# A decode block on one core: 21 tiny probe loads on SP's queue and three 17-partition loads issued by GpSimd

## The chip, the cores and the metric

The kernel runs on one core of one Trainium2 chip. The time is device microseconds of one execution. Before the change the median of two runs is 185.91 us (185.82 and 186.01). Traces come from one profiled execution; times inside it count from the start of its span.

## The reference

One block of a transformer at decode: two sequences, one token each, 640 channels, modulated by a condition `c`. In short:

```python
mod = silu(c) @ w_mod                      # (2,640) @ (640,3840): sa, ca, ga, sb, cb, gb
h = layernorm(x) * (1 + ca) + sa
q = h @ wq                                 # 32 heads of 192
k, v = k_cache[:, :, -1024:], v_cache[:, :, -1024:]
o = softmax(q @ k.T * 192 ** -0.5) @ v
x = x + ga * (o @ wo)
h = layernorm(x) * (1 + cb) + sb
x = x + gb * ((gelu(h @ w_gate) * (h @ w_up)) @ w_down)
```

All tensors are bf16. With one token a sequence, every weight and every cached key and value is used once. The kernel reads 76.88 MB: `w_mod` 4.9 MB, `wq` and `wo` 7.9 MB each, keys and values 25.2 MB each, and 5.9 MB for the feed-forward part.

## The kernel before, in words

All big loads go into one buffer of 128 partitions, `arena`, at places written out by hand (`place`, with `tiles` for the pieces of the caches; `HS` is half a slot of 64 x 192 elements). They are issued on SP's queue in this order: `w_mod`; `wq`; for sequence 0 the K tiles 0 and 1 (64 positions a partition) and 2 (128 positions), V tile 0; K tile 0 of sequence 1; V tile 1 of sequence 0; K tile 1 of sequence 1; the two V tiles of sequence 1; `wo`; `w_gate`; `w_up`; and `w_down` in three parts of 8, 3 and 1 rows. The function `pump` issues the next load as soon as every earlier load that overlaps it in `arena` has been consumed, so an SP issue waits on the semaphore of the engine that reads the old contents. The first load is moved ahead of the program's opening barrier. A load puts 128 rows on the DMA engines, 8 rows an engine, one packet a row (38 to 61 KB for the big ones).

The computation follows the loads. `w_mod` gives the modulation (L454), `wq` the queries (L486), which are copied to all partitions (`qbc`). For each K tile DVE multiplies 16 positions at a time with the query (L512, `d_mul`), PE sums over channels through an identity matrix (L524, `p_reduce`), and DVE ends the sums (L531, `c_sum`). The softmax (L537 to L554) is followed by `weights_v`: DVE spreads the weights of 64 positions over the 32 heads into one of the two halves of `Em` (L561), and PE multiplies them with the V tile (L575, `p_pv`). After the last V tile come the selection of heads (L616), a row of matmuls into an unused bank that keep the clock up (`keep_clock`, L408, which read `Em`), `wo` (L634), the second layer norm, `w_gate` and `w_up` (L655), and `w_down` (L675), whose three parts each wait for their own load. Two DVE operations (L681, L683) make the output, and ACT issues the store (L685). SP waits for the store at the end (L698).

GpSimd sets up constants in the first 7.3 us (memsets and masks; the last are the `zsel` selects, L374) and does nothing after. ACT issues two small loads at the start: `c` (2 partitions of 1280 bytes) and `x` (8 partitions of 320 bytes). All issues pass through the helper `k_dma`, so all have line L290 in the profile.

Dependences are tracked by key: `S.op` and `S.dma` take lists of keys read and written, and `resolve` turns them into semaphore waits, of which it leaves out those that an earlier wait of the same engine covers. Each engine runs its list in order.

`Em` (128 partitions, 2 x 64 x 32 bf16) is written for the first time by L561, at 87.85 us in the trace.

Of the kernel before, what the change touches and what calls it, by code (L numbers as in the profile page):

```python
# [8 lines left out]
BF16 = mybir.dt.bfloat16  # L9
# [110 lines left out]
def bass_adaLN_cond__sliding_block_cached__geglu_ffn__decode_kernel(  # L120
# [51 lines left out]
    WD_SPLIT = [(0, 8), (8, 3), (11, 1)]  # L172
# [15 lines left out]
    with es:  # L188
        S = _Sched(nc, es)
        sb = lambda name, shape, dt: es.enter_context(nc.sbuf_tensor(name, shape, dt))  # L190
# [10 lines left out]
        for kind, b, t, z in tiles:  # L201
            j0, n = (K_SPLIT if kind == "k" else V_SPLIT)[b][t]
# [25 lines left out]
        maskE = sb("maskE", [P, H], BF16)  # L228
# [29 lines left out]
        Em = sb("Em", [P, 2, JE, H], BF16)  # L258
# [22 lines left out]
        def bank(k):  # L281
            return ("bank", k)
# [6 lines left out]
        def k_dma(dst, src):  # L289
            return lambda e: e.dma_start(dst, src)  # L290

        items = list(place)
        assert items[0] == ("wm", 0)
        queue = {"next": 0, "done": set(), "ops": {}}

        def overlap(x, y):
            (a, m), (b, n) = place[x], place[y]
            return a < b + n and b < a + m

        def keys(it, lo=0, width=None):  # L300
            o, n = place[it]
            width = n - lo if width is None else width
            assert lo + width <= n
            return [("ar", z) for z in range((o + lo) // UNIT, -(-(o + lo + width) // UNIT))]

        def view(it, lo=0, width=None):
            o, n = place[it]
            width = n - lo if width is None else width
            return arena[:, o + lo:o + lo + width]

        def source(it):
            kind = it[0]
            if kind == "wm":
                return w_mod.rearrange("(p k) n -> p (k n)", k=KT)
            if kind == "wq":
                k0, n = WQ_SPLIT[it[1]]
                return A_wq.rearrange("(p k) n -> p (k n)", k=KT)[:, k0 * NQ:(k0 + n) * NQ]
            if kind == "wo":
                t0, n = WO_SPLIT[it[1]]
                return A_wo.rearrange("(p t) n -> p (t n)", t=NT)[:, t0 * D:(t0 + n) * D]  # L320
            if kind == "wg":
                return B_w_gate.rearrange("(p k) n -> p (k n)", k=KT)
            if kind == "wu":
                k0, nk = WU_SPLIT[it[1]]
                return B_w_up.rearrange("(p k) n -> p (k n)", k=KT)[:, k0 * F:(k0 + nk) * F]
            if kind == "wd":
                r0, nr = WD_SPLIT[it[1]]
                return B_w_down.rearrange("(p r) n -> p (r n)", r=FC)[:, r0 * D:(r0 + nr) * D]
            b, (j0, n) = it[1], span[it]
            src = A_k_cache if kind == "k" else A_v_cache  # L330
            return src[b][:, K0:Sk, :].rearrange("h (x j) d -> h x j d", x=XQ)[:, :, j0:j0 + n, :].rearrange("h x j d -> h x (j d)")

        def pump(*consumed):
            queue["done"].update(consumed)
            while queue["next"] < len(items):
                n = queue["next"]
                it = items[n]
                if not all(x in queue["done"] for x in items[:n] if overlap(x, it)):
                    break
                queue["ops"][it] = S.dma("sp", k_dma(view(it), source(it)), sem_of[it], writes=keys(it), name="ld_%s" % "_".join(str(z) for z in it))  # L340
                queue["next"] += 1

        pump()
        wm_dma = queue["ops"][("wm", 0)]
        S.op("pool", lambda e: e.memset(xr[:, :], 0.0), writes=["xr"], name="xr0")
# [4 lines left out]
        for nm, t in (("scT", scT), ("oT", oT)):  # L350
# [6 lines left out]
             reads=["ones_f"], writes=["ident_f"], name="ident_f")  # L357
        S.op("pool", lambda e: e.tensor_copy(out=ident_b[:, :], in_=ident_f[:, :]),
             reads=["ident_f"], writes=["ident_b"], name="ident_b")
        S.op("pool", lambda e: e.memset(aT[:, 0:RB], 0.0), writes=["aT0"], name="aT0")  # L360
        S.op("pool", lambda e: e.memset(selq[:, :, :], 0.0), writes=["selq"], name="selq0")
        for b in range(B):
# [4 lines left out]
                 reads=["ones_b"], writes=[("selt", b)], name="selt%d" % b)  # L367
            S.op("pool", lambda e, b=b: e.tensor_copy(out=selq[:, b, :].rearrange("p (u x) -> p u x", x=SQW)[:, :, 0:P].rearrange("p u (i v) -> p u i v", i=NR)[:, :, :, 0:XQ],
                                                      in_=selt[:, b, :].rearrange("p (i x) -> p i x", x=XQ).unsqueeze(1).broadcast_to([P, HB, NR, XQ])),
                 reads=[("selt", b), "selq"], writes=["selq"], name="selq%d" % b)  # L370
        S.op("pool", lambda e: e.memset(scl[:, :], SCALE), writes=["scl"], name="scl")
        S.op("pool", lambda e: e.memset(zsel[:, :, :], 0.0), writes=["zsel"], name="zsel0")
        for i in range(2):
            S.op("pool", lambda e, i=i: e.affine_select(out=zsel[:, :, :], in_=zsel[:, :, :], pattern=[[-P, 2], [-1, ZW]],  # L374
                                                        compare_op=ALU.not_equal, fill=1.0, base=DD - 1 - 2 * P * i, channel_multiplier=DD),
                 reads=["zsel"], writes=["zsel"], name="zsel%d" % (i + 1))

        S.op("dve", lambda e: e.memset(ps[:, 0:4, :], 0.0), writes=[bank(k) for k in range(4)], name="init_Q")
        S.op("dve", lambda e: e.memset(ps[:, 6:8, :], 0.0), writes=[bank(k) for k in range(6, 8)], name="init_O")
        S.op("dve", lambda e: e.tensor_reduce(out=mask_h[:, :], in_=ident_f[:, :].rearrange("p (h x) -> p h x", x=XQ), axis=AX.X, op=ALU.add),  # L380
             reads=["ident_f"], writes=["mask_h"], name="mask_h")
        S.op("dve", lambda e: e.tensor_reduce(out=st32[:, :], in_=ident_f[:, :].rearrange("p (i m) -> p m i", m=32), axis=AX.X, op=ALU.add),
             reads=["ident_f"], writes=["st32"], name="st32")
        S.op("dve", lambda e: e.tensor_reduce(out=halfsel[:, :], in_=st32[:, :].rearrange("p (h m) -> p h m", h=2), axis=AX.X, op=ALU.add),
             reads=["st32"], writes=["halfsel"], name="halfsel")
# [3 lines left out]
             reads=["st32"], writes=["selstat"], name="selstat")  # L389
# [3 lines left out]
        def c_T(e):  # L393
            last = None
            for j in range(KT):
# [4 lines left out]
             reads=[bank(BK_T)], writes=["scT"], name="silu")  # L400
        S.op("dve", lambda e: e.tensor_copy(out=X[:, :], in_=xr[:, :]),  # L401
             reads=["xr"], writes=["X"], name="x_f32")
# [26 lines left out]
        def ln_mod(tag, opc_idx, s_idx, dst_bf):  # L429
# [15 lines left out]
             reads=["mask_h"], writes=["maskc"], name="maskc")  # L445
        S.op("dve", lambda e: e.tensor_copy(out=maskE[:, :], in_=mask_h[:, :]), reads=["mask_h"], writes=["maskE"], name="maskE")

        for half in range(2):
            def f(e, half=half):
                last = None  # L450
                for k in range(KT):
# [9 lines left out]
                 reads=[bank(half)], writes=[("modR", half)], name="mod%d_evac" % half)  # L461
            S.op("dve", lambda e, half=half: e.tensor_scalar(out=opc[:, half, :], in0=modR[:, 3 * half + 1, :], scalar1=1.0, scalar2=None, op0=ALU.add),  # L462
                 reads=[("modR", half)], writes=[("opc", half)], name="opc%d" % half)
            if half == 0:
                ln_mod("ln1", 0, 0, hT)
        pump(("wm", 0))

        def out_rows(src, key, dst_t, name):
# [9 lines left out]
        for w, (k0, nk) in enumerate(WQ_SPLIT):  # L478
            def f(e, w=w, k0=k0, nk=nk):
                last = None  # L480
                wv = view(("wq", w)).rearrange("p (k i n) -> p k i n", k=nk, i=NR)
                for kk in range(nk):
                    k = k0 + kk
                    for n in range(NQB):
                        for i in range(NR):
                            last = e.matmul(ps[32 * i:32 * i + B, n, :], lhsT=hT[:, k, 0:RM:RB], rhs=wv[:, kk, i, n * QW:(n + 1) * QW],  # L486
                                            start=(k == 0), stop=(k == KT - 1), tile_position=(0, 32 * i))
                return last
            S.op("pe", f, reads=["ln1_out"] + keys(("wq", w)), writes=[bank(n) for n in range(NQB)], name="q1_%d" % w)
            pump(("wq", w))  # L490
        for n in range(NQB):
            if n % 2 == 0:
                S.op("act", lambda e, n=n: e.activation(out=qrow[:, n * QW:(n + 1) * QW], in_=ps[:, n, :], func=ACTF.Copy),
                     reads=[bank(n)], writes=[("qrow", n)], name="q1_evac%d" % n)
            else:
                S.op("dve", lambda e, n=n: e.tensor_copy(out=qrow[:, n * QW:(n + 1) * QW], in_=ps[:, n, :]),  # L496
                     reads=[bank(n)], writes=[("qrow", n)], name="q1_evac%d" % n)
        for b in range(B):
            def f(e, b=b):
                last = None  # L500
                for u in range(HB):
# [5 lines left out]
                 reads=[bank(BK_T + b)], writes=[("qbc", b)], name="q2_evac%d" % b)  # L507
# [49 lines left out]
        def weights_v(it):  # L557
            b, (j0, n) = it[1], span[it]
            for j in range(j0, j0 + n, JE):
                z = j // JE % 2  # L560
                S.op("dve", lambda e, z=z, j=j: e.tensor_tensor(out=Em[:, z, :, :], in0=E_sb[:, b, j:j + JE].unsqueeze(2).broadcast_to([P, JE, H]),  # L561
                                                                in1=maskE[:, :].unsqueeze(1).broadcast_to([P, JE, H]), op=ALU.mult),
                     reads=[("E", b), "maskE"], writes=[("Em", z)], name="Em%d_%d" % (b, j))

        def p_pv(it):
            b, (j0, n) = it[1], span[it]
# [19 lines left out]
        for n, it in enumerate(tiles):  # L586
            kind, b, t = it
# [24 lines left out]
        def p_sel(e):  # L612
            last = None
            for dd in range(DD):
# [10 lines left out]
             reads=[bank(BK_OT), "oT"], writes=["oT"], name="oT")  # L625
# [3 lines left out]
        def wo_f(e):  # L629
            last = None  # L630
            wv = view(("wo", 0)).rearrange("p (t i n) -> p t i n", t=NT, i=NR)
            for t in range(NT):
# [9 lines left out]
             reads=[bank(2), ("modR", 0)], writes=["lnt"], name="ga_attn")  # L642
        S.op("dve", lambda e: e.tensor_tensor(out=X[:, :], in0=lnt[:, :], in1=X[:, :], op=ALU.add),
             reads=["lnt", "X"], writes=["X"], name="x1")
# [4 lines left out]
        def ffn_gu(bk, wv, name, splits):  # L649
            for ci, (k0, nk, key) in enumerate(splits):  # L650
# [11 lines left out]
             reads=[bank(0)], writes=["gl"], name="gelu")  # L662
# [3 lines left out]
             reads=[bank(1), "gl"], writes=["aR"], name="geglu")  # L666
        S.op("dve", lambda e: e.transpose(aT[:, RB:RB + FC * 32], aR[:, :]), reads=["aR"], writes=["aT"], name="aT")
        for ci, (r0, nr) in enumerate(WD_SPLIT):
            def f(e, r0=r0, nr=nr):
# [12 lines left out]
             reads=[bank(BK_OT), "go"], writes=["fin"], name="gb_y")  # L682
        S.op("dve", lambda e: e.tensor_tensor(out=finb[:, :], in0=fin[:, :], in1=xo[:, :], op=ALU.add),  # L683
             reads=["fin", "xo"], writes=["finb"], name="outR")
        S.dma("act", k_dma(out[:, 0, :].rearrange("b (u n) -> u b n", n=OC), finb[0:P:SB, :]),  # L685
              sem_out, reads=["finb"], name="st_out")
# [9 lines left out]
        del body[n0:]  # L696
        body[entry:entry] = moved
        S.emit("sp", nc.sync, tail=lambda e: e.wait_ge(sem_out, 16))  # L698
        S.emit("pool", nc.gpsimd)
        S.emit("act", nc.scalar)  # L700
        S.emit("dve", nc.vector)
        S.emit("pe", nc.tensor)
# [42 lines left out]
```

## Time and profile before

| what | value |
|---|---|
| median of 2 runs | 185.91 us (185.82, 186.01) |
| span of the profiled execution | 184.6 us (the page gives no other time of it) |
| DVE, PE, PE weight loads, ACT, GpSimd busy | 107.3, 106.4, 28.9, 14.4, 6.1 us |
| mean granted TensorE clock | 0.884 |
| HBM read | 76.88 MB, 417 GB/s over the span |
| DMA packets | 2495, of which 310 under 512 bytes |
| code fetches seen on the DMA engines | six of 16 KB on queue 8, one of 8 KB on queue 14 in the span |

A busy share is an average over stages with different limits, so the stages are looked at one by one. A DMA share of 1.00 says that all 16 engines had a packet in hand all the time. The chain of waits is followed back from the last instruction: at each step it names what released the work, which can be a transfer that itself had waited its turn behind others.

### The profile page before, as it was taken

The page shows a single profiled execution, that of the slowest core. Times are in us where ns is not written, and L with a number is a line of the kernel's source. Part 1 is how long each engine was busy: PE and PEld are TensorE (multiplying, and loading weights), DVE is VectorE, ACT ScalarE, POOL GpSimd, SP SyncE. Part 2 cuts the span into 40 slices and gives each one's busy share as a digit, 9 for nine tenths or more (in the row PEclk, how much of TensorE's full clock was granted, in tenths as well). Part 3 has the DMA queues.
Part 4 walks back from the last instruction along what each step waited for, and adds up shares of the span by engine and source line. Part 5 has one row for each costly group of instructions (what it writes and reads, how often), then busy time and mean ns, then how long its engine had stood idle before and what let it go on. Part 6 is the DMA issues. An engine that isn't in the chain of part 4 may idle for free.

```text
span 184.6 us, 1862 instructions
## 1 busy us (share of the span) xinstructions
PE 106.4 (58%) x960; PEld 28.9 (16%) x693; DVE 107.3 (58%) x105; ACT 14.4 (8%) x27; POOL 6.1 (3%) x23
## 2 busy tenths in 40 slices
PE   0019000948663096662499665946662499898833
PEld 0012000120000000001260001500001356405213
DVE  6022200049993488965993999489975838300631
ACT  2041100050000000001000000000001000220410
POOL 8400000000000000000000000000000000000000
PEclk9999955699999859999589999999998559999995
DMA  8999998999898989899898989898999999979991
GB/s 292 492 496 426 426 426 357 442 426 488 368 501 352 501 362 501 384 460 469 384 490 366 490 362 490 373 490 373 479 405 447 506 443 426 426 316 403 434 376 40
DMA packets 2495, 76.99 MB, mean 417 GB/s; under 512 B 310, under 2 KB 440, under 8 KB 568
## 3 DMA queue, kind: packets, MB, share of 16 engines
q1 hardware_dynamic: 2448, 76.87, 97.1%
q8 instruction: 6, 0.10, 0.2%
q10 hardware_dynamic: 40, 0.01, 0.0%
q14 instruction: 1, 0.01, 0.0%
HBM read 76.88 MB, written 0.00 MB: 417 GB/s over the span
## 4 chain that ended last, share of the span: by engine, by line
DMA 58%; DVE 24%; PE 16%; ACT 1%; issue 1%; SPq 0%
DMA arena<-in_A_k_cache_dram 36%; DMA arena<-in_B_w_down_dram 14%; DVE arena L512 14%; PE ps L575 8%; DMA arena<-in_w_mod_dram 8%; DVE S_sb L531 6%; PE ps L524 3%; DVE Em L561 2%; PE ps L454 2%; PE ps L675 1%; DVE negm L541 1%; ACT E_sb L549 1%; PE ps L552 1%; PE ps L545 0%; DVE M L537 0%
## 5 line engine op out<-in xcount | busy, mean ns | idle before, releaser
L524 PE MATMUL ps<-arena,ident_b 128*128 128x512 bf16 x192 | 48.9, 395 | 29.2 <-DVE arena L512 29.2
L512 DVE TENSOR_TENSOR arena<-arena,qbc 128x3072 bf16<-128x3072 bf16 x32 | 54.8, 1750 | 10.2 <-DMA arena<-in_A_k_cache_dram 8.5
L575 PE MATMUL ps<-arena,Em 128*64 128x384 bf16 x256 | 26.1, 374 | 5.6 <-DVE Em L561 5.6
L531 DVE TENSOR_REDUCE S_sb<-ps 128x32 f32<-128x1024 f32 x16 | 19.5, 1218 | 7.1 <-PE ps L524 7.1
L575 PEld LDWEIGHTS ps<-arena,Em 128*64 128x64 bf16 x256 | 16.2, 126 | 30.7 <-DVE Em L561 22.0
L561 DVE TENSOR_TENSOR Em<-E_sb,maskE 128x2048 bf16<-128x2048 bf16 x8 | 18.0, 2282 | 3.9 <-PE ps L575 3.9
L486 PE MATMUL ps<-arena,hT 128*2 128x512 bf16 x60 | 5.1, 517 | 14.0 <-DMA arena<-in_A_wq_dram 14.0
L496 DVE CAST qrow<-ps 128x512 bf16<-128x512 f32 x1 | 0.7, 691 | 17.4 <-PE ps L486 17.4
L539 PEld LDWEIGHTS ps<-ident_f,M 128*1 128x1 f32 x2 | 0.2, 79 | 61.1 <-DVE M L537 61.1
L408 PE MATMUL ps<-Em,ident_b 128*128 128x512 bf16 x41 | 9.3, 379 | 0.0
L641 DVE TENSOR_TENSOR lnt<-ps,modR 128x160 f32<-128x160 f32 x1 | 0.3, 323 | 12.7 <-PE ps L634 12.7
L549 ACT ACTIVATE E_sb<-S_sb,nbias 128x256 bf16<-128x256 f32 x2 | 1.0, 507 | 66.7 <-DVE nbias L547 66.7
L454 PE MATMUL ps<-arena,scT 128*17 128x480 bf16 x40 | 4.2, 602 | 2.1 <-DMA arena<-in_w_mod_dram 2.1
L582 ACT ACTIVATE On<-ps,rden 128x384 bf16<-128x384 f32 x2 | 1.2, 580 | 49.2 <-PE ps L575 49.2
L634 PEld LDWEIGHTS ps<-arena,oT 128*17 128x17 bf16 x192 | 3.3, 91 | 7.4 <-DMA arena<-in_A_wo_dram 7.4
L396 PE MATMUL ps<-ident_b,crow 2*128 2x2 bf16 x5 | 0.4, 177 | 6.5 <-DMA crow<-in_c_dram 6.5
L634 PE MATMUL ps<-arena,oT 128*17 128x160 bf16 x192 | 3.5, 233 | 0.6 <-DMA arena<-in_A_wo_dram 0.6
L417 PE MATMUL ps<-st,selstat 128*128 128x2 f32 x4 | 0.9, 298 | 4.9 <-ACT sqj L413 4.9
L401 DVE CAST X<-xr 128x160 f32<-128x160 bf16 x1 | 0.2, 243 | 5.8 <-DMA xr<-in_A_x_dram 5.8
L486 PEld LDWEIGHTS ps<-arena,hT 128*2 128x2 bf16 x20 | 0.6, 110 | 18.4 <-issue 18.4
L462 DVE TENSOR_SCALAR opc<-modR 128x160 f32<-128x160 f32 x2 | 0.5, 244 | 4.7 <-ACT modR L459 4.7
L655 PE MATMUL ps<-arena,h2T 128*9 128x384 bf16 x40 | 2.0, 326 | 1.9 <-DMA arena<-in_B_w_up_dram 1.3
(86 smaller groups left out, 51.1 us busy)
## 6 DMA issues: line engine op xcount, KB each, us to landing
arena<-in_A_v_cache_dram SPq DMA_DIRECT2D x4, 6144.0 KB, 26.3
arena<-in_A_k_cache_dram SPq DMA_DIRECT2D x3, 6144.0 KB, 37.5
arena<-in_A_wq_dram SPq DMA_DIRECT2D x1, 7680.0 KB, 31.5
arena<-in_A_wo_dram SPq DMA_DIRECT2D x1, 7680.0 KB, 29.2
arena<-in_A_k_cache_dram SPq DMA_DIRECT2D x2, 3072.0 KB, 42.2
arena<-in_w_mod_dram SPq DMA_DIRECT2D x1, 4800.0 KB, 14.2
arena<-in_B_w_gate_dram SPq DMA_DIRECT2D x1, 1920.0 KB, 21.2
arena<-in_B_w_up_dram SPq DMA_DIRECT2D x1, 1920.0 KB, 22.8
```

What stands on the lines that cost most here:

```text
L408: last = e.matmul(ps[:, BK_T, :], lhsT=ident_b[:, :], rhs=Em[:, 0, 0:512 // H, :].rearrange("p j h -> p (j h)"), start=True, stop=True)
L454: last = e.matmul(ps[32 * i:32 * i + RM, half, 0:MH].rearrange("p (m n) -> p m n", n=DR), lhsT=scT[:, k, :], rhs=wv[:, 3 * half:3 * half + ...
L486: last = e.matmul(ps[32 * i:32 * i + B, n, :], lhsT=hT[:, k, 0:RM:RB], rhs=wv[:, kk, i, n * QW:(n + 1) * QW], start=(k == 0), stop=(k == K ...
L512: S.op("dve", lambda e: e.tensor_tensor(out=kt, in0=kt, in1=qbc[:, b, :].unsqueeze(1).broadcast_to([P, JC, Dh]), op=ALU.mult), reads=[("qb ...
L524: last = e.matmul(o_ap, lhsT=ident_b[:, :], rhs=kt[:, :, t * GC:(t + 1) * GC], start=(t == 0), stop=(t == NCH - 1))
L531: S.op("dve", lambda e: e.tensor_reduce(out=S_sb[:, b, 2 * JC * pair:2 * JC * (pair + 1)], in_=ps[:, 2 * z:2 * z + 2, :].rearrange("p k (j ...
L541: S.op("dve", lambda e: e.tensor_reduce(out=negm[:, b, :].rearrange("p (h x) -> p h x", x=XQ), in_=ps[0:1, BK_T, 0:P].rearrange("p (h x) - ...
L549: S.op("act", lambda e: e.activation(out=E_sb[:, b, :], in_=S_sb[:, b, :], func=ACTF.Exp, scale=SCALE, bias=nbias[:, b:b + 1], accum_out=d ...
L561: S.op("dve", lambda e, z=z, j=j: e.tensor_tensor(out=Em[:, z, :, :], in0=E_sb[:, b, j:j + JE].unsqueeze(2).broadcast_to([P, JE, H]), in1= ...
L575: last = e.matmul(ps[64 * i:64 * i + 2 * H, BK_O, 0:ON], lhsT=Em[:, z, 2 * jp:2 * jp + 2, :].rearrange("p j h -> p (j h)"), rhs=view(it, l ...
L634: last = e.matmul(ps[32 * i:32 * i + RM, 2, 0:DR], lhsT=oT[:, t, :], rhs=wv[:, t, i, :], start=(t == 0), stop=(t == NT - 1), tile_position ...
L655: last = e.matmul(ps[32 * i:32 * i + GM, bk, 0:FT], lhsT=h2T[:, k, 0:RM:2], rhs=wv[:, k, i * FT:(i + 1) * FT], start=(k == 0), stop=(k == ...
```

## The change

Three things are added and nothing is taken away.

1. Tiny loads on SP's queue. `probe(eng, k)` loads the first 16 elements (32 bytes) of the first k rows of `w_mod` into k partitions of a new buffer `prb`, each with a semaphore and a column of its own. Three of them (4, 8 and 12 partitions) follow the load of K tile 2 of sequence 0, three more that of V tile 0 of sequence 1, and fifteen (17 and 2 to 15 partitions) follow the last part of `w_down`.
2. Three loads issued by GpSimd behind its last set-up instruction. Each takes 17 rows of `w_mod`, two pieces a row, into 17 partitions of `Em` (from partition 0, 32 and 64), with pieces of 1024, 768 and 1280 elements (2048, 1536 and 2560 bytes). The values are not used: `Em` is written over by L561, which is made to wait for all three loads.
3. At the end GpSimd waits for all 24 semaphores.

```diff
+        prb = sb("prb", [17, 24, 16], BF16)
+        probes = []
+
+        def probe(eng, k):
+            n = len(probes)
+            sem = S.sem("d_prb%d" % n)
+            probes.append(sem)
+            S.dma(eng, k_dma(prb[0:k, n, :], w_mod[0:k, 0:16]), sem, writes=[("prb", n)], name="prb%d" % n)
...
                 queue["ops"][it] = S.dma("sp", k_dma(view(it), source(it)), sem_of[it], writes=keys(it), ...)
                 queue["next"] += 1
+                if it in (("k", 0, 2), ("v", 1, 0)):
+                    for k in (4, 8, 12):
+                        probe("sp", k)
+                if it == ("wd", len(WD_SPLIT) - 1):
+                    for k in (17,) + tuple(range(2, 16)):
+                        probe("sp", k)
...
+        for z, n in enumerate((1024, 768, 1280)):
+            sem_z = S.sem("d_swz%d" % z)
+            probes.append(sem_z)
+            emv = Em[:, :, :, :].rearrange("p z j h -> p z (j h)")
+            S.dma("pool", k_dma(emv[32 * z:32 * z + 17, :, 0:n], w_mod[0:17, 0:4 * 640].rearrange("p (z m) -> p z m", z=2)[:, :, 0:n]), sem_z,
+                  writes=[("Em", 0), ("Em", 1)] if z == 0 else [("swz", z)], name="swz%d" % z)
...
-                     reads=[("E", b), "maskE"], writes=[("Em", z)], name="Em%d_%d" % (b, j))
+                     reads=[("E", b), "maskE"], writes=[("Em", z), ("swz", 1), ("swz", 2)], name="Em%d_%d" % (b, j))
...
-        S.emit("pool", nc.gpsimd)
+        S.emit("pool", nc.gpsimd, tail=lambda e: [e.wait_ge(x, 16) for x in probes])
```

## The prediction

> **What bounds the kernel now.** I read the cores' spans first (one core, 184.6 us at clock 0.884), then the DMA rows of the page, then a table of stages, then the end in order of time, then SP's waits. The page:
>
> ```profile
> DMA  8999998999898989899898989898999999979991
> ...
> q1 hardware_dynamic: 2448, 76.87, 97.1%
> ...
> DMA 58%; DVE 24%; PE 16%; ACT 1%; issue 1%; SPq 0%
> ```
>
> The chain gives DMA only 58%, which looks like a kernel that alternates between loading and computing. The busy row and the stages say otherwise (columns: us, busy time of each engine, PE clock, DMA share, GB/s):
>
> ```profile
> core 0: us, PE busy (x) PEld busy (x) DVE busy (x) ACT busy (x) POOL busy (x), PEclk, DMA share, GB/s
> 1.00:40.00 39.00, 11.46 (x122) 4.00 (x83) 7.77 (x24) 5.95 (x11) 5.70 (x19) 0.82 1.00 426
> 40.00:140.00 100.00, 62.94 (x329) 9.07 (x137) 82.29 (x56) 2.79 (x5) 0.00 (x0) 0.93 1.00 433
> 140.00:180.00 40.00, 30.17 (x416) 14.21 (x378) 16.72 (x25) 5.65 (x11) 0.00 (x0) 0.86 0.98 420
> 180.00:181.90 1.90, 1.48 (x92) 1.50 (x95) 0.00 (x0) 0.00 (x0) 0.00 (x0) 0.50 0.26 92
> 181.90:184.60 2.70, 0.31 (x20) 0.10 (x8) 0.48 (x2) 0.00 (x0) 0.00 (x0) 0.50 0.01 1
> ```
>
> From 1 to 180 us the 16 DMA engines have no gap: 433 GB/s, or 27 GB/s each. The links of the chain that name DVE or PE are buffers given back early enough. The bound is the one stream on SP's queue, plus 2.7 us of tail behind its last byte.
>
> The last stretch matters most here, because the engines don't end together. The trace marks when each of a load's 16 engines finishes. For the first part of w_down the marks are 178.33 to 178.58 (nine engines), then 179.07, 179.53, 179.88, 179.94, 180.01, 180.03 and 180.28. Its matmuls start on the last mark:
>
> ```profile
> 180.42 1.79 PE L675 MATMUL ps<-arena,aT 128*25 128x80 bf16 x96 [2.20 <-DMA arena<-in_B_w_down_dram]
> 182.25 0.24 DVE L681 TENSOR_TENSOR fin<-ps,go 128x80 f32<-128x80 f32 x1 [2.75 <-PE ps L675]
> 182.53 0.24 DVE L683 TENSOR_TENSOR finb<-fin,xo 128x80 bf16<-128x80 f32 x1
> 182.80 0.66 ACTq L290 DMA_DIRECT2D out_dram<-finb  x1
> ```
>
> So the slowest engine sets the end, and nine engines are 1.70 to 1.95 us ahead of it. Why they differ can be read from the DMA records: each 16 KB code fetch (43, 98, 150, 166 and 173 us) sits on one engine for 1.0 to 1.1 us, and that engine's next weight packet is about 0.5 us longer (1411 against 912 ns after the first). Each fetch makes one more engine late; they don't pile on one. A delay that one engine gets is never made up.
>
> **The change, part by part.** *The three GpSimd loads.* Each is 17 partitions x 2 pieces, 34 pieces of 2048, 1536 and 2560 bytes: 70, 52 and 87 KB, 209 KB in all. Spread over 16 engines that would be 209 KB / 433 GB/s = 0.5 us. But 17 partitions need not spread. The nearest rows are ACT's two small loads: c (2 partitions) used two engines, x (8 partitions, 4 column groups) four. A common divisor of the shape fits both, and 17 has none but itself and 1: one engine per load. A piece costs what its size costs: packets of 1280 bytes took 55 ns and those of 3840 bytes 149 ns, so 8 ns + 0.0367 ns per byte, which gives 83, 64 and 102 ns. By 34 pieces: 2.8, 2.2 and 3.5 us on an engine.
>
> Do the three loads share an engine? By the rows of c and x they would, as x uses c's two engines again. By the rows of the code fetches, one-packet transfers of another queue, each goes elsewhere. GpSimd's queue is in neither set. I take three engines, since a fetch is the nearer case (a whole transfer on one engine), and keep both ends for the range: all on one is 8.5 us there, all spread is 0.5 us everywhere.
>
> The Trainium skill (DMA: Bandwidth & Descriptors, "Why a DMA increments its semaphore by 16 and not by 1") has both answers for GpSimd's queue: k consecutive engines from a round-robin cursor, k the largest common divisor up to 16, but also an exception in which a copy gets ceil(partitions/16) partitions per engine. The first is three engines for these loads, the second nine engines with two partitions each; by the second the sum would be about 1.0 us on nine engines.
>
> With three engines, the end moves by the largest of (delay minus lead). All on quick engines: 3.5 minus 1.7 to 1.95, +1.6 us. If the 3.5 falls on one of the six engines within 0.75 us of the last: +2.7 to +3.5. If the 2.8 falls on one of those instead: about +2.4. Weighted by how many engines are of each sort (10 and 6 of 16) the mean and the middle are both +2.4 us.
>
> That this delay passes through: w_down's matmuls, L681, L683 and the store follow its landing with nothing in between, so the tail stays 2.7 us. Upstream, the third K tile's landing (62.34 us) moves by up to 3.5 us, and with it the chain that gives back buffers. Load issues lead the quick engines by 104.4 - 97.45 = 6.9 us (last K tile) and 118.9 - 113.51 = 5.4 us (third V tile), so the stream doesn't run dry below that.
>
> *The wait on DVE.* The first Em write (L561) now waits for all three loads; queued behind it on DVE are a second Em, the K products and the sums, and PE waits for these:
>
> ```profile
> 87.85 4.47 DVE L561 TENSOR_TENSOR Em<-E_sb,maskE 128x2048 bf16<-128x2048 bf16 x2
> ```
>
> When are the loads there? ACT's pieces took turns with the stream: c's piece at 4.50, its mark at 5.96, then x's at 7.39 and 8.82, one piece for each 1.42 us weight packet. GpSimd issues at 7.3 us. 34 pieces and a mark are 35 turns: 3 in the rest of w_mod, 8 each in wq, the two half K tiles and the third K tile, so about 61 us. 27 us of cover; cost 0. What these waits cost themselves (SP's row: 17 ns each) is under the 6.9 us lead.
>
> *Tiny loads on SP.* 21 issues. The costliest issue row is 0.54 us on SP. Three behind the third K tile end near 20.6 us, and the next load waits for its buffer until 37.58; three behind the third V tile end near 115.7, and the next issues at 119.66. Cover 4 us or more, and were it gone that next load starts only at 133.4 on the engines.
>
> ```profile
> SPq L290 <- PE ps L524: 78.6, 4, 28.6
> SPq L290 <- PE ps L575: 34.2, 4, 13.8
> SPq L698 <- DMA out_dram<-finb: 28.4, 1, 28.4
> ```
>
> The last 15 take the place of SP's 28 us wait for the store. On an engine a piece of 320 bytes took 20 ns and a mark 9 ns: 3 x 29 = 0.09 us a batch on the lowest engines, 0.17 us ahead of the end. Between 0 and 0.17 counts, if the latest engine is a low one; I take 0. The last batch lands behind w_down: at most 31 pieces and 15 marks, 0.8 us, done near 182.6, with the store's packets at 184.1. GpSimd's 24 waits at the end have nothing behind them and are over before SP's; if that cover went, up to 0.8 us.
>
> *Code.* More instructions could bring one more fetch: 0 to 1.5 us on one engine. I take 0; SP runs 20 instructions now and GpSimd 32.
>
> Sum: +2.4 us. The page gives the profiled execution's span alone, 184.6; the two runs are 1.3 us above it (median 185.91), which I leave as it is. 184.6 + 2.4 + 1.3 = 188.3 us, +1.3%. With three engines the time is 187.5 to 189.5.
>
> **The rivals.**
> *Spread, 0.28.* The loads don't sit on one engine each. Dealt as evenly as 17 rows go over 16 engines, no engine gets more than two rows of a load: 12 pieces, 4 x (83 + 64 + 102) = 1.0 us, on up to nine engines (17 rows in twos), one of the late ones very likely among them: +0.5 to +1.0, 186.4 to 186.9. For it: nothing in the trace shows GpSimd's placing. Against: ACT's rows.
>
> *All on one engine, 0.08: slower.* 103 pieces and marks are 105 turns. By 87.85 us about 50 are done (35 by 61, then 8 per 14.5 us), so L561 waits. The point where this decides is about 50 turns on one engine. The stream goes on until 104.4, when it lacks the last K tile's buffer; the rest of the pieces then go back to back, done near 113; Em and PV (2.3 + 7.3) give that buffer back at 123 instead of 97.45, and the stream stands for some 20 us: 206 us. If a turn carries several pieces, the wait goes and 8.5 us minus the lead stays: +6.7 to +8.5, 192.6 to 194.4. The skill (same page, "Queues, rings and completion order") speaks for several: it says an engine drains a whole packet of some 9 to 17 descriptors before it switches.
>
> *Each switch costs the stream, 0.13: slower.* After a fetch the next weight packet lost 0.5 to 0.66 us; after ACT's 320 and 1280 bytes it lost nothing (1420 ns each). Pieces of 1.5 to 2.5 KB are nearer to the second, hence the small chance. From 0.06 us a turn (34 turns, +2 us more) it passes 2%; at 0.1 us 191.7, at 0.5 us 205.
>
> *Nothing moves, or faster, 0.06.* The loads land on engines with enough lead, or code fetches fall more kindly: 185.0 to 186.2. More is impossible: the lateness is 1.95 us in all, and the bytes take 178 us at 433 GB/s.
>
> **How the numbers follow.** Forecast 0.45, 188.3 us. From 185.8 to 192.5 lie the forecast, the spread, most of the last rival and half of the switching one: 0.45 + 0.28 + 0.05 + 0.06 = 0.84. 2%, about what a measurement of this kernel tells from no change, is 189.6: slower gets the two slow rivals and a tenth of the forecast, 0.26; faster 0.01; the rest, 0.73, is within.
>
> **What would show it.** Right: GpSimd's queue with 102 pieces and some 209 KB, on three engines; three engines late by 2 to 3.5 us more in every load from the third K tile on, and w_down landing near 182.7; tail 2.7 us; DMA share 1.00 to 180; L561 without a DMA wait. Wrong: the loads' pieces on nine engines or on one; L561 waiting for Em's loads; weight packets longer after each piece; a gap in the DMA share; or a tail over 2.8 us because of the 15 last probes.

## The result and the profile after

The changed kernel takes 191.38 us (191.34 and 191.43) against 185.91: 1.029 times the time before, interval 1.026 to 1.032. Slower was forecast, but by 2.4 us and not 5.5. The span is 190.0 us; what lies around it is 1.4 us, 1.3 before. Two kernels below had one execution each far above their others (194.36 us of the one with 16 partitions, which is also the one profiled, and 367.27 us of the one with a single GpSimd load and no last tiny loads); the ratios leave these two out, and without them the medians are 188.20 and 188.43 us.

The page after, DMA rows, queues (packets, MB, share) and chain:

```profile
DMA  9999999999999999999999999999999999979940
...
q1 hardware_dynamic: 2800, 76.88, 95.4%
q0 software_dynamic: 784, 0.22, 0.5%
...
DMA 59%; DVE 21%; PE 18%; issue 1%; ACT 1%; SPq 0%
```

The chain hardly changed. What stands out is GpSimd's queue, q0: 784 packets where 102 pieces were issued, with 0.22 MB. Only 46 of them carry data (17 of 4096 bytes, 11 of 4608 and one of 1536, 17 of 5120: two or three pieces each, the one of 1536 a single piece). The others have 4, 8 or 12 bytes. They lie on *all* the other engines: for every piece that one engine moves, 4 bytes on each of the 15 others, grouped like the data packets, and at the end of a load a mark on all 16 (46 x 16 + 3 x 16 = 784).

The stages, in the columns shown before the change; the last two stretches are cut at w_down's last mark:

```profile
1.00:40.00 39.00, 10.22 (x107) 2.72 (x67) 7.66 (x23) 5.11 (x10) 8.70 (x22) 0.78 1.01 423
40.00:140.00 100.00, 62.97 (x323) 10.14 (x152) 76.56 (x53) 3.63 (x8) 0.00 (x0) 0.88 1.01 426
140.00:180.00 40.00, 30.97 (x394) 12.85 (x338) 20.29 (x21) 3.91 (x10) 0.00 (x0) 0.91 0.99 423
180.00:187.30 7.30, 3.74 (x130) 2.25 (x128) 2.85 (x10) 1.74 (x2) 0.00 (x0) 0.84 0.42 162
187.30:190.00 2.70, 0.38 (x24) 0.17 (x12) 0.48 (x2) 0.00 (x0) 0.00 (x0) 0.50 0.01 1
```

The engines are still never idle until 180 us (share 0.99 to 1.01), yet they move 426 GB/s in place of 433 from 40 to 140 us: packets take longer, no gap has opened. The tail is the same 2.7 us. New is a stretch of 7 us at the end in which ever fewer engines still work (share 0.42): one of them is far behind. The end follows it as before:

```profile
185.89 1.79 PE L696 MATMUL ps<-arena,aT 128*25 128x80 bf16 x96 [2.20 <-DMA arena<-in_B_w_down_dram]
187.73 0.24 DVE L702 TENSOR_TENSOR fin<-ps,go 128x80 f32<-128x80 f32 x1 [2.74 <-PE ps L696]
188.00 0.24 DVE L704 TENSOR_TENSOR finb<-fin,xo 128x80 bf16<-128x80 f32 x1
188.28 0.66 ACTq L290 DMA_DIRECT2D out_dram<-finb  x1
```

The marks of the 16 engines in the trace say where the 5.5 us come from (us; first, ninth and last engine to finish a load):

| load | before: first, ninth, last | after: first, ninth, last |
|---|---|---|
| wq | 31.59, 31.72, 32.31 | 31.76, 32.12, 33.77 |
| K tile 0 | 38.89, 39.03, 39.62 | 39.28, 39.72, 42.74 |
| K tile 2 | 60.72, 60.87, 62.34 | 61.76, 62.49, 65.30 |
| V tile 0 | 75.25, 75.40, 76.86 | 76.90, 78.00, 82.57 |
| first part of w_down | 178.33, 178.58, 180.28 | 180.04, 182.00, 185.76 |

Nearly all of it is lost before 83 us and kept to the end. The quickest engine is 1.71 us later, though no data of the GpSimd loads touched it, and the last is 5.72 us behind the quickest in place of 1.95: 1.71 + 5.72 - 1.95 = 5.48 us.

The tiny loads name the engines: one of k partitions leaves its marks on the k lowest. Behind w_down the one of 2 partitions is done at 185.08 and 185.40, and 3 partitions add 187.47. So the slowest is the third engine, which has the third and largest load. Issue to landing of the three, in us:

```profile
Em<-in_w_mod_dram POOLq DMA_DIRECT2D x1, 85.0 KB, 71.4
Em<-in_w_mod_dram POOLq DMA_DIRECT2D x1, 68.0 KB, 34.2
Em<-in_w_mod_dram POOLq DMA_DIRECT2D x1, 51.0 KB, 45.3
```

They land at 41.8, 54.0 and 81.0 us, one after the other: the 16 marks of the first come at 37.80 to 41.77 us, those of the second at 49.25 to 53.95, those of the third at 72.55 to 80.97, so on every engine a load's packets stand ahead of those of the next. The wait in front of Em, in the timeline of DVE, is still free, with 9.7 us to spare (the line names no idle time before it):

```profile
90.72 4.62 DVE L582 TENSOR_TENSOR Em<-E_sb,maskE 128x2048 bf16<-128x2048 bf16 x2
```

### The profile page after: what moved, and what is told of

Same layout as the page of the kernel before. It is cut to its first block, busy times and chain, and to the rows that moved or that the text cites. A ratio compares the mean times of both kernels' runs of the same rounds, so it can differ in the third digit from the quotient of the medians.

```text
span 190.0 us, 1901 instructions
## 1 busy us (share of the span) xinstructions
PE 108.3 (57%) x960; PEld 28.1 (15%) x693; DVE 107.9 (57%) x105; ACT 14.4 (8%) x27; POOL 9.1 (5%) x26
## 4 chain that ended last, share of the span: by engine, by line
DMA 59%; DVE 21%; PE 18%; issue 1%; ACT 1%; SPq 0%
DMA arena<-in_A_k_cache_dram 39%; DMA arena<-in_B_w_down_dram 13%; DVE arena L533 12%; DMA arena<-in_w_mod_dram 8%; PE ps L596 7%; PE ps L545 6%; DVE S_sb L552 6%; DVE Em L582 2%; PE ps L475 2%; PE ps L696 1%; DVE negm L562 1%; ACT E_sb L570 1%; PE ps L573 1%; DVE M L558 0%; PE ps L566 0%
## 5 line engine op out<-in xcount | busy, mean ns | idle before, releaser
L545 PE MATMUL ps<-arena,ident_b 128*128 128x512 bf16 x192 | 52.4, 421 | 32.1 <-DVE arena L533 32.0
L596 PE MATMUL ps<-arena,Em 128*64 128x384 bf16 x256 | 24.8, 360 | 5.7 <-DVE Em L582 5.7
L596 PEld LDWEIGHTS ps<-arena,Em 128*64 128x64 bf16 x256 | 15.6, 121 | 30.0 <-DVE Em L582 22.2
L696 PE MATMUL ps<-arena,aT 128*25 128x80 bf16 (+1 forms) x96 | 1.8, 266 | 2.2 <-DMA arena<-in_B_w_down_dram 2.2
```

What stands on the lines that cost most here:

```text
L545: last = e.matmul(o_ap, lhsT=ident_b[:, :], rhs=kt[:, :, t * GC:(t + 1) * GC], start=(t == 0), stop=(t == NCH - 1))
L596: last = e.matmul(ps[64 * i:64 * i + 2 * H, BK_O, 0:ON], lhsT=Em[:, z, 2 * jp:2 * jp + 2, :].rearrange("p j h -> p (j h)"), rhs=view(it, l ...
L696: last = e.matmul(ps[32 * i:32 * i + m, BK_OT, CY:CY + OC], lhsT=aT[:, 32 * fc + a:32 * fc + a + m], rhs=wv[:, i, h, :], start=(fc == WD_S ...
```

## The experiments

Each is an edit of the changed kernel; times are medians, each beside runs of the kernel before on the same chip (185.79 to 185.96 us). The main theory is called padding: the 4-byte pieces on the other engines, which the forecast didn't have.

**One half of the change at a time.** Without the GpSimd loads:

```diff
-        for z, n in enumerate((1024, 768, 1280)):
+        for z, n in ():
```

> The 21 tiny loads alone, no GpSimd loads. Padding theory (each GpSimd load puts a 4-byte piece on the 15 other engines for every piece of its own, and these small packets and the load's own engine make up the whole loss): 186.0 us, +0 to +0.2, and the quick engines finish the first part of w_down at 178.3 to 178.5 as before. Rival (the probes in the middle of the stream make part of the loss): +1 us or more, the quick engines later than 178.8.

185.94 us, ratio 1.0008 (0.9998 to 1.0017). The 21 tiny loads alone cost next to nothing. They also say how the three lowest engines stand without the loads: about 0.3, 1.4 and 0.3 us behind the quickest in w_down. The third belongs to the quick ones.

Without the tiny loads:

```diff
-                if it in (("k", 0, 2), ("v", 1, 0)):
+                if False:
...
-                if it == ("wd", len(WD_SPLIT) - 1):
+                if False:
```

> The three GpSimd loads alone, no tiny loads. Padding theory: quick engines 1.6 us later than before in w_down (46 small packets an engine plus 3 marks, 34 ns each), one engine some 5 us behind these, 190.3 to 191.2 us. Rival (probes make part of the loss, the loads cost what I forecast): 188 to 189 us. If only the crowding of the third load's packets between the probes is the probes' part (packets of 340 to 470 ns in place of 200), it is 0.5 to 1 us below the changed kernel.

190.64 us, ratio 1.026 (1.0243 to 1.0277); quickest engine 179.90 in w_down, 1.57 us late, last one 5.15 us behind it. The GpSimd loads make nearly all of the loss, more than the forecast alone. Together with them the tiny loads seem to cost 0.7 us that they don't cost by themselves; the intervals overlap (the changed kernel's is 1.0262 to 1.0322), but the last mark of w_down's first part agrees, 185.06 us here and 185.76 there.

**Largest load first.**

```diff
-        for z, n in enumerate((1024, 768, 1280)):
+        for z, n in enumerate((1280, 1024, 768)):
```

> As the changed kernel, with pieces of 1280, 1024 and 768 elements in place of 1024, 768 and 1280, so that the largest load comes first. Padding theory, with the loads on the three lowest engines in turn and a switch that costs nothing beside the packets of wq but 30 to 80 ns beside those of the caches: the largest one is the cheaper for it, the last engine is 4 to 4.6 us behind the quick ones, the quick ones 1.7 us late: 189.8 to 190.4 us. Rival (the third engine is slow by itself, whatever it loads, or the largest load costs the same anywhere): 191.2 to 191.5 us.

190.52 us, ratio 1.0258 (1.0242 to 1.0273), a little above the expected range (0.4 us of it lies outside the span, for the reason shown with the single loads below). The lowest engine is now the last one (2-partition marks 185.68 and 186.22 behind w_down, where w_down ends at 185.85): the loads go to the three lowest engines in the order of issue, and the engine of the largest load is the last in either order. It is 4.1 us behind the quickest, not 5.7. The lateness doesn't follow the bytes alone: the engines of the 68 and the 51 KB load both end about 3.8 us behind the quickest. Beside wq's packets a 5 KB packet costs its own 0.2 us and hardly more (the weight packet behind it took 2282 ns, 2267 without); beside the cache tiles, as in the changed kernel, the next packet takes 1896 ns in place of 1818.

**Padding by itself, once and twice.** Pieces of 32, 24 and 40 bytes, still 17 partitions:

```diff
-        for z, n in enumerate((1024, 768, 1280)):
+        for z, n in enumerate((16, 12, 20)):
```

> As the changed kernel, with pieces of 16, 12 and 20 elements (32, 24, 40 bytes) in the GpSimd loads, still 17 partitions and 34 pieces each. In the changed kernel a GpSimd packet holds two or three pieces, 4.1 to 5.1 KB. Theory (the other engines get a small packet for each packet): 34 short pieces fit in one packet, so the other engines get one small packet and one mark a load, quick engines +0.1 to 0.3 us, 186.0 to 186.5 us. Rival (a small packet for each piece or each two pieces, or a fixed cost of a 17-partition load): 17 or more turns a load, quick engines +1.2 us or more, 187.2 us or more.

186.92 us, ratio 1.0052 (1.0037 to 1.0067): between the two. The queues:

```profile
q1 hardware_dynamic: 2800, 76.88, 97.1%
q8 instruction: 6, 0.10, 0.2%
q0 software_dynamic: 96, 0.01, 0.1%
```

All 34 pieces went into one packet, as the theory had it: 3 loads x 16 engines x (packet and mark) = 96. But the cost didn't fall with the packets. The padding packet has 136 bytes, 34 times 4, and the wq packet behind it took 2544 ns in place of 2267: 0.28 us, or 8 ns a piece. So one packet of 34 small pieces costs far more than one of two, behind which the changed kernel lost 0 to some 40 ns. That the price goes by pieces is argued from this one load shape: no run changes the number of pieces of a load, and whether the price lies in the pieces or in 15 engines writing at once, no run tells. Doubled to six loads:

```diff
-        for z, n in enumerate((1024, 768, 1280)):
+        for z, n in enumerate((16, 12, 20, 16, 12, 20)):
...
-            S.dma("pool", k_dma(emv[32 * z:32 * z + 17, :, 0:n], ...
+            S.dma("pool", k_dma(emv[32 * (z % 3):32 * (z % 3) + 17, :, z // 3 * 64:z // 3 * 64 + n], ...
...
-                     ..., writes=[("Em", z), ("swz", 1), ("swz", 2)], ...
+                     ..., writes=[("Em", z)] + [("swz", i) for i in range(1, 6)], ...
```

> Six GpSimd loads of 17 partitions with pieces of 32, 24 and 40 bytes in place of three, 186.92 us. Theory (what a 17-partition load costs the other 15 engines goes by its pieces, 4 bytes for each, some 8 ns apiece: 34 pieces were 0.28 us on the next weight packet): twice the loss, quick engines 1.9 to 2.2 us late in w_down, 187.8 to 188.2 us. Rival (a first use of the queue, paid once): 186.9 to 187.2 us.

187.98 us, ratio 1.0108 (1.0093 to 1.0123), quickest engine 1.95 us late:

```profile
q0 software_dynamic: 192, 0.02, 0.2%
```

1.0 us for three loads, 2.1 for six, with next to no data moved (6.5 KB by six loads, and 0.02 MB by the queue): padding is a cost of its own, paid on every engine for each load.

**One load, by either queue.** Only the largest, by ACT and by GpSimd:

```diff
-        for z, n in enumerate((1024, 768, 1280)):
+        for z, n in enumerate((1280,)):
...
-            S.dma("pool", k_dma(emv[32 * z:...
+            S.dma("act", k_dma(emv[32 * z:...
```

> Of the three loads only the largest (17 partitions, pieces of 2560 bytes), issued by ACT. Theory (only GpSimd's queue fills up the other engines): no small packets elsewhere, quick engines at 178.3 to 178.6 in the first part of w_down, the lowest engine 3.6 to 4.6 us behind them: 187.5 to 188.7 us. Rival (ACT's queue fills up as well): quick engines 0.4 us later.

> The same single load, issued by GpSimd. Theory: 17 packets of 8 bytes and a mark on each other engine, quick engines 0.3 to 0.6 us late, the load's engine 3.6 to 4.4 us behind these: 187.9 to 189.2 us, 0.3 to 0.6 us above the one that ACT issues. Rival (no difference between the queues but the packing of pieces in pairs): the same as ACT's or below.

188.94 us (ratio 1.0164, 1.0144 to 1.0183) and 189.08 (1.017, 1.0155 to 1.0185): ACT's above its range, GpSimd's near the top of its own, and only 0.14 us apart where 0.3 to 0.6 was expected. The queues, ACT's (q10) and GpSimd's (q0):

```profile
q10 hardware_dynamic: 75, 0.09, 0.1%
q0 software_dynamic: 288, 0.09, 0.2%
```

Without this load q10 has 40 packets, so ACT's load makes 35: its 34 pieces and one mark, and nothing on the other engines. GpSimd's has 17 packets of data, 16 marks and 255 packets of 8 bytes, 17 on each of 15 engines. Up to V tile 0 the quickest engine is 0.07 us late with ACT and 0.40 with GpSimd, as the theory has it. At w_down it is 178.69 and 178.95 us, and the last engine 182.80 and 182.89: the times of this pair alone would not show that padding costs anything. On the load's own engine ACT moved 34 pieces of 102 to 111 ns, 3.6 us, close to the forecast's 3.5, and GpSimd 17 packets of some 200 ns, 3.4 us.

In both the time is 1.7 us above the span, where it had been 1.3 to 1.4. Here the lowest engine is the last, and behind its w_down come all fifteen tiny loads: 184.41 to 187.12 us with GpSimd's load, 2.7 us where the forecast had 0.8. Two kernels without this batch:

```diff
-                if it == ("wd", len(WD_SPLIT) - 1):
+                if False:
```

> The kernel with GpSimd's one load (189.08 us) without the fifteen tiny loads behind w_down. There the lowest engine is the slowest, has all fifteen behind its last weight packet, and the time is 1.7 us over the span in place of 1.3. Theory (GpSimd's wait for them ends the kernel): 188.5 to 188.7 us, 1.3 us over its span. Rival (they are hidden, the 0.4 us has another cause): 189.0 to 189.2 us.

> The changed kernel without the fifteen tiny loads behind w_down. In its profile the slowest engine's last one is done at 189.57 us, before the store (190.01), and the time is 1.4 us over the span as before the change. Theory (hidden there, since only 13 of them touch the slowest engine): 191.2 to 191.4 us. Rival (they delay the end in the changed kernel too): 190.9 us or less.

188.54 us with the one load (ratio 1.0141, 1.0124 to 1.0158), 1.3 above its span: 0.5 to 0.65 us less. Some 0.4 of that lies outside the span, as expected if GpSimd's wait for the last tiny loads ends the kernel there; the other 0.2 is the store, whose last mark came 2.90 us behind w_down's with the tiny loads and comes 2.69 without. With all three loads 190.85 us (ratio 1.0266, 1.0249 to 1.0283, against 1.0292, 1.0262 to 1.0322): in the rival's range and not the theory's, but the intervals overlap, and a share of 0 to 0.5 us is all that can be said.

**Where tiny loads and GpSimd's meet.** Only the first batch left out:

```diff
-                if it in (("k", 0, 2), ("v", 1, 0)):
+                if it == ("v", 1, 0):
```

> The changed kernel without the three tiny loads behind the third K tile; the later ones stay. Theory (where these tiny loads meet the GpSimd loads, near 62 to 66 us, the turns come closer together and weight packets are 90 to 200 ns longer instead of 40): 190.6 to 190.9 us, as without any tiny loads (190.64). Rival (the later tiny loads make the 0.7 us): 191.2 to 191.4 us.

190.88 us, ratio 1.0268 (1.0251 to 1.0284). The 17 largest GpSimd packets take 3.4 us together, as without any tiny loads, and 4.5 us in the changed kernel, where from 62 to 66 us eight of them come with only tiny loads between them and take 200 to 470 ns. By the last mark of w_down's first part (185.22 us, against 185.76 in the changed kernel and 185.06 without any tiny loads) this meeting is most of the 0.7 us. The times alone don't show it: the intervals overlap, and the kernel without the last batch, in which the meeting is still there (4.4 us for the 17 packets), takes 190.85 us.

**16 partitions.** One row on every engine, so nothing to pad:

```diff
-            S.dma("pool", k_dma(emv[32 * z:32 * z + 17, :, 0:n], w_mod[0:17, 0:4 * 640]...
+            S.dma("pool", k_dma(emv[32 * z:32 * z + 16, :, 0:n], w_mod[0:16, 0:4 * 640]...
```

> As the changed kernel, but the GpSimd loads take 16 partitions in place of 17 (16/17 of the bytes). Padding theory: 16 divides over all engines, so each gets one row, two pieces of each load, no padding: three packets and marks an engine, about 0.25 us for the data and 0.2 for six switches, 186.2 to 186.6 us, all engines equally late. Rival (a GpSimd queue costs the stream whatever the shape, by its descriptors or its issue): 188 us or more.

188.27 us, ratio 1.0125 (1.0108 to 1.0142). Better than 17 by 3.1 us, and a miss all the same: 6 packets an engine can't be 2.4 us by their bytes. In place of padding, each weight packet behind a GpSimd packet is longer (second row of the table below, a kernel that takes the same time). Three kernels looked for the reason: rows to every eighth partition (`emv[z:128:8]`), rows from every fortieth of w_mod (`w_mod[0:640:40]`), and ACT as issuer.

> As the kernel with 16 partitions (188.27 us), but the 16 rows go to every eighth partition instead of 16 side by side. Destination theory (the weight packet behind each GpSimd packet was 0.36 to 0.76 us longer because 16 engines wrote into neighbouring partitions at once): half or less of the loss, 186.4 to 187.4 us. Rival (what costs is the switch, or the reading): 188.0 to 188.4 us, and the packets behind are as long as before.

> As the kernel with 16 partitions (188.27 us), but the 16 rows of w_mod are every fortieth instead of the first 16. Source theory (16 engines read at once from 123 KB side by side): half or less of the loss, 186.4 to 187.4 us. Rivals (destination, or the switch itself): 188.0 to 188.4 us.

> As the kernel with 16 partitions (188.27 us), but ACT issues the three loads. Theory that the loss comes from what is written or read where: 187.6 to 188.4 us. Rival (GpSimd's queue, with its packets of two or three pieces, makes it): each piece takes a turn of its own without loss as c and x did, 186.2 to 186.7 us.

| kernel | us | ratio (interval) | weight packet behind a packet of 4096, 3072, 5120 bytes: longer by |
|---|---|---|---|
| every eighth partition | 187.17 | 1.0071 (1.0045 to 1.0098) | 0.12, 0.19, 0.33 us |
| every fortieth row | 188.17 | 1.0120 (1.0105 to 1.0135) | 0.42, 0.41, 0.67 us |
| ACT issues | 188.33 | 1.0133 (1.0113 to 1.0152) | single pieces, 0.2 to 0.3 us each |

The queue of every fortieth row, for all of this shape: 96 packets, of which 48 are marks.

```profile
q0 software_dynamic: 96, 0.20, 0.3%
```

Neither the rows read nor the queue changes the time; where the rows are written does, and every eighth partition halves the loss, 1.2 us in place of 2.4. Of these 1.2, 0.64 us is on the packets behind, and 0.5 is the data by the packets' own times (159, 125 and 222 ns), twice what was expected for it. The reading is that sixteen engines writing side by side hold each other up; that they crowd on a way into SBUF is not shown.

## Why the prediction was half right

- *The bound, the tail and the engines' lead:* right. DMA share 1.0 to 180 us, tail 2.7 us before and after, a delay on one engine kept from 83 us to the end, no gap in the stream. (433 GB/s is the figure for 40 to 140 us; the stages on either side have 426 and 420.)
- *One engine per load, three engines:* right, against the rows of c and x, where the second load took the first one's engines again. The Trainium skill (DMA: Bandwidth & Descriptors, "Why a DMA increments its semaphore by 16 and not by 1") has consecutive engines from a cursor for GpSimd's queue, which these runs agree with; its exception, two partitions an engine, doesn't show here. The rivals that spread the loads or put all on one engine fall.
- *2.8, 2.2 and 3.5 us on an engine:* right for the data alone (3.4 and 3.6 us for the largest in the single-load runs).
- **The step that failed: "By 34 pieces: 2.8, 2.2 and 3.5 us on an engine", taken as all that the loads cost.** The other engines were priced at nothing. In the changed kernel they pay 1.7 us for padding (1.0 in the kernel with tiny pieces, where it stands alone); the third load's engine pays the data, 4.5 us where the tiny loads meet it in place of 3.4, and 17 longer weight packets, 17 x 78 ns = 1.3 us; it is spared its own load's padding, 17 small packets of 9 ns with some 36 ns behind each, 0.8 us. That is 5.0 us more than the quick engines, where the marks have 5.72 with 0.3 of its own lateness; 0.4 us I can't assign. So where the forecast had 3.5 minus a lead of 1.7 to 1.95, the marks have 1.71 + 5.72 minus the lead of 1.95. The third engine is one of the quick ones, so the forecast's own case was +1.6 us, and its weighted +2.4 was the nearer to 5.5 by luck.
- *"Each switch costs the stream":* a rival at 0.13, and partly what happened, at 0.08 us a data packet and 0 to 0.05 us a padding packet, not as the main cause. Its row, ACT's small pieces after which nothing was lost, was a row beside w_mod; beside the caches, with GpSimd's larger packets, it didn't hold.
- *27 us of cover for Em:* only 9.7. I let the three loads run side by side; padding puts them in line. Still free.
- *Last batch of tiny loads, 0.8 us, hidden:* 2.7 us on the lowest engine. Hidden in the changed kernel or nearly so, not hidden where the lowest engine is the last.
- *Tiny loads on SP, code fetches:* right by themselves. Six fetches of 16 KB as before, and the tiny loads alone change nothing that can be measured; what they cost where they meet GpSimd's loads, up to 0.7 us, was not foreseen. The costliest issue on SP is 0.61 us and not 0.54, which changes none of its covers.

No kernel here beats the one before: all of them add transfers to a stream without gaps.

## What to carry to other kernels

Where a load stream leaves the DMA engines no gap, look at the marks of the 16 engines one by one: the last engine sets the time, and a delay on it is never made up. A GpSimd load of 17 partitions, the one such shape tried here, cost twice, its bytes on one engine and a small piece on all the others for each of its pieces; price both, and the weight packet that stands behind each. Before adding a small load at all, count its packets on the engine that is last, not its bytes over 16.

## What the runs showed of the hardware that was not expected

- A 17-partition load from GpSimd puts 4 bytes on each of the 15 other engines for each of its pieces (784 packets for 102 pieces); from ACT it doesn't (35 packets for 34 pieces). 34 of them in one packet make the next 60 KB packet 0.28 us longer.
- In pairs or threes these padding packets cost nothing behind them beside wq up to 24 us, and 20 to 60 ns each from 28 us on, beside the last of wq and the cache tiles. Why is open.
- 16 engines that write 16 neighbouring partitions at once lose 0.4 to 0.7 us a packet; on every eighth partition 0.1 to 0.3 us.
- GpSimd put two or three pieces of 1.5 to 2.5 KB in a packet, up to 5 KB, and 34 pieces of 24 to 40 bytes in one. The Trainium skill (DMA: Bandwidth & Descriptors, "Queues, rings and completion order") has typical packets of 9 to 17 descriptors; here it was 2, 3 or 34 pieces, the more the smaller they were.
